# Moving one dense matmul ahead of the first weighing part in units 18 to 30, and reordering the tail's output products

## The chip, the core and the metric

The kernel runs on one core of a Trainium2 chip. The metric is device microseconds (us) of one execution; each time quoted is the median of several runs. TensorE does the matmuls, VectorE, ScalarE and GpSimd the elementwise work, and SyncE issues most DMAs.

## The reference, cut to what matters

```python
xn = layernorm(x)                                     # x: 1 x 2048 x 1024, bf16
return x + attention(xn, wq, wk, wv, wo, beta) + token_mlp(xn, w1, b1, w2, b2)

def attention(x, ...):                                # 32 heads of 32, four segments of 512 tokens
    for s in range(4):
        p = softmax(q_s k_s^T * scale + causal_mask)
        a_dot = p v_s                                 # inside the segment
        a_mem = phi(q_s) M / (phi(q_s) z + 1e-6)      # memory of the earlier segments
        outs.append(g * a_mem + (1 - g) * a_dot)      # g = sigmoid(beta), per head
        M, z = M + phi(k_s)^T v_s, z + sum(phi(k_s))
    return concat(outs) @ wo
# [... the token MLP: two matmuls with a gelu between ...]
```

## The kernel before

The token MLP runs first. The attention then goes through 32 *units*: a unit is one segment and one group of four heads. Each unit makes *score products* (TensorE), which ScalarE exponentiates and GpSimd masks. *Weighing* multiplies the masked weights by the values, and is done for the previous unit, in three parts (0, 1, 2), so that TensorE needn't wait. Between these stand *dense* matmuls (projections and output products, eight matmuls of 512 columns to a job), which depend on nothing recent and fill TensorE's waits. An even unit has a third score product, which covers blocks of two units.

TensorE writes to eight banks: 0 to 3 hold scores, 4 and 5 weighing results, 6 and 7 dense jobs in turn. A bank can be written again only when the engine that empties it has finished. One order of instructions is fixed for each engine when the program is built. A dense job of the output product is emptied by an addition on VectorE (`fin`), and a weighing part by a copy on VectorE (`ost`). VectorE works through them in the order in which they were emitted.

```python
    def wo_job(self, c, half):          # one output product: 8 matmuls, then an addition on VectorE
        # [... mm(b, j): matmul j of the job into bank b ...]
        def end(b):
            dst, R = self.fin[c % 4][:, half * 512:(half + 1) * 512], self.R_fin[c % 4][half]
            self.fw.op("dve", lambda e: e.tensor_tensor(dst, self.bank(b), dst.bitcast(F16), op=ALU.add),
                       reads=[self.R_bank[b], R], writes=[R])
            # [... with the second half: store to out, load the next fin ...]

    def dense(self, n, side=True):      # the next n dense matmuls
        # [... cut ...]
            with fw.group(reads=reads(), writes=[self.R_bank[b]]):
                for i in range(at, stop):
                    mm(b, i)
            if stop == 8:
                end(b)                  # the job is complete: its evacuation is emitted here
                self.jobs.popleft()

    def logits(self, u, step):          # score product: matmuls into banks 0 to 3, one exponential out of them
        # [... cut ...]
        reads = [R for v in units for R in (self.R_kT[v % 3], self.R_qT[v % 3])]
        with fw.group(reads=reads, writes=self.R_bank[0:4]):
            # [... four or eight matmuls of 32 rows ...]
        fw.op("act", lambda e: e.activation(dst, src, ACT.Exp, scale=SCALE), reads=self.R_bank[0:4], ...)
        # [... a causal mask on GpSimd for each diagonal block ...]

    def attention(self):
        # [... cut ...]
            if u < 10 or u >= 14 and total <= 26:
                cuts = self.cut(total, (0, 4, 2, 4, 1, 13, 8) if even else (7, 3, 2, 4, 1, 15))
            else:
                cuts = self.cut(total, (0, 4, 2, 2, 2, 14, 8) if even else (7, 3, 2, 2, 2, 16))
            self.dense(cuts[0])
            self.logits(u, 0)                        # first score product
            self.dense(cuts[1], end)
            self.weigh(u - 1, 0)                     # first weighing part
            self.dense(cuts[2], False)
            self.weigh(u - 1, 1)
            self.dense(cuts[3], False)
            self.weigh(u - 1, 2)                     # third part: the bank of part 0 again
            # [... VectorE's steps on the results, queued ...]
            self.dense(cuts[4])
            self.logits(u, 1)                        # second score product
            if even:
                self.dense(cuts[5])
                self.logits(u, 2)                    # third score product
            self.dense(...)                          # the rest
```

```python
    def _waits(self, es, reads, writes, extra=()):
        # [... need: one token for each semaphore, in the order in which it was met ...]
        for t in need.values():
            es.wait_tok(t)
```

After the last unit, the tail does the last segment's output products, numbered 0 to 7, into all eight banks. Slice 6 of each needs the DMA that transposes unit 30's output (`oT<-o_s` in the profile), and slice 7 needs unit 31's.

```python
        def product(n, j0, j1, cols=((0, 512),)):    # slices j0 to j1 of product n
            i, h, b = n // 2, n % 2, (0, 1, 2, 3, 6, 7, 5, 4)[n]
            # [... the matmuls; after slice 7 an addition on VectorE and a store ...]
        product(0, 0, 6)
        product(1, 0, 6)
        self.weigh(u, 0)
        self.weigh(u, 1)
        product(2, 0, 6)
        self.weigh(u, 2)
        # [... VectorE's steps of unit 31 ...]
        product(3, 0, 6)
        for n in range(3):
            product(n, 6, 7)
        product(4, 0, 7)
        self.o_transpose(u, 4)
        product(3, 6, 7)
        product(5, 0, 7)
        for n in range(6):
            product(n, 7, 8)
        product(6, 0, 8)
        product(7, 0, 8, ((0, 256), (256, 384), (384, 512)))
```

## Time and profile before

| | before |
|---|---|
| time, median of 3 runs (first measurement) | 654.29 us |
| span of the profiled execution | 652.22 us |
| first score product of unit 18 to that of unit 31 | 97.59 us |
| first score product of unit 31 to the start of the last matmul | 20.43 us |
| start of the last matmul to the end | 2.90 us |

These lines of the page of the kernel before give each engine's busy time (share of the span, count of instructions), the granted clock in 40 slices (9 is 90% or more), the queue of instruction fetches (packets, MB), and the engines' shares of the chain of work that ended last.

```profile
span 652.2 us, 11204 instructions
...
PE 646.7 (99%) x4611; PEld 303.1 (46%) x4611; DVE 439.9 (67%) x829; ACT 281.5 (43%) x305; POOL 154.9 (24%) x181
...
PEclk9999999999999999999999999999999999999999
...
q8 instruction: 36, 0.59, 0.4%
...
PE 90%; DVE 4%; DMA 2%; ACT 1%; POOL 1%; issue 1%; DVEq 0%
```

TensorE (PE) bounds the kernel: it is busy for 99% of the span at full clock. What can move the time is a gap between matmuls, or the end behind the last one.

These lines are the timeline of the kernel before: start, length, engine, line, operation, out<-in, count, and in brackets the idle time of that engine before it and its inferred releaser. They come from unit 20, from unit 26 (first score product and first weighing part) and from the tail. PEld is TensorE's weight load, SPq a DMA issue on SyncE.

```profile
547.90 0.74 DVE L1466 TENSOR_TENSOR o_s<-prod 128x512 bf16<-128x512 bf16 x1
...
548.56 0.56 DVE L1414 CAST ost<-ps_all 128x396 bf16<-128x396 f32 x1
...
549.04 0.68 DVE L1306 TENSOR_TENSOR fin<-ps_all,fin 128x512 bf16<-128x512 f32 x1
549.17 0.47 PEld L199 LDWEIGHTS ps_all<-vA,pT 128*128 128x128 bf16 x16 [0.42 <-DVE ost L1414]
...
588.48 1.88 ACT L1363 ACTIVATE pT<-ps_all 128x2048 bf16<-128x2048 f32 x1 [0.79 <-PE ps_all L199]
...
590.48 0.13 PEld L199 LDWEIGHTS ps_all<-qT,kT 32*128 32x128 bf16 x4 [0.49 <-issue]
590.50 0.40 PE L199 MATMUL ps_all<-qT,kT 32*128 32x512 bf16 x4
...
590.91 0.82 PE L199 MATMUL ps_all<-wv,xnT 128*128 128x512 bf16 x3
...
591.92 0.25 PE L199 MATMUL ps_all<-vA,pT 128*128 128x33 bf16 x4 [0.19 <-POOL pT L1367]
...
633.89 2.75 PE L199 MATMUL ps_all<-wo,oT 128*128 128x512 bf16 x12 [0.24 <-ACT pT L1363]
...
636.15 0.34 SPq L221 DMA_DIRECT2D out_dram<-fin  x1
636.53 0.92 SPq L221 DMA_DIRECT2D fin<-out_dram  x1
...
637.49 1.19 SPq L221 DMA_TRANSPOSE oT<-o_s  x1
...
640.46 0.98 PEld L199 LDWEIGHTS ps_all<-wo,oT 128*128 128x128 bf16 x6 [0.49 <-DMA oT<-o_s]
```

In unit 20, VectorE empties the bank of part 0 (548.56) directly behind `o_s`, then does the output addition; the third weighing part follows at 549.17. In unit 26 the first weighing part waits for GpSimd. In the tail TensorE waits for an exponential at 633.89 and for the transposing DMA at 640.46. A load's bracket holds more than a loss, because a load normally overlaps the matmul before it. The gaps quoted below are therefore starts of matmuls, less the 0.216 us that a matmul of 512 columns takes.

### The profile page before, as it was taken

How to read it: one execution, taken by the hardware profiler on the slowest of the kernel's cores; microseconds unless marked ns; L12 is line 12 of the kernel's file. 1: busy time of each engine (PE TensorE's matmuls, PEld its weight loads, DVE VectorE, ACT ScalarE, POOL GpSimd, SP SyncE). 2: the span in 40 equal slices, each digit the busy share in tenths (PEclk: the TensorE clock that was granted, in tenths of full speed). 3: DMA queues.
4: the chain of work that ended last, by engine and by line, in shares of the span. 5: the costliest groups of instructions: out<-in, count | busy, mean ns of one | idle time of the engine just before them, and what ended most of it. 6: DMA issues, size and time to landing. Idle time of an engine off the chain costs nothing.

```text
span 652.2 us, 11204 instructions
## 1 busy us (share of the span) xinstructions
PE 646.7 (99%) x4611; PEld 303.1 (46%) x4611; DVE 439.9 (67%) x829; ACT 281.5 (43%) x305; POOL 154.9 (24%) x181
## 2 busy tenths in 40 slices
PE   9999999999999999999999999999999999999998
PEld 3444444444444444444444444444545444454444
DVE  6975775665655673745637325767898988887895
ACT  7542232232210000111101047778767788888760
POOL 2500000000011220120201203434333445544450
PEclk9999999999999999999999999999999999999999
DMA  8804242242498937629263956979644576355424
GB/s 300 217 0 130 65 116 79 65 124 70 129 265 216 231 96 210 171 87 258 66 193 116 257 136 156 190 182 227 124 120 109 152 164 144 90 115 123 114 81 138
DMA packets 190123, 95.00 MB, mean 146 GB/s; under 512 B 108664, under 2 KB 176248, under 8 KB 190072
## 3 DMA queue, kind: packets, MB, share of 16 engines
q1 hardware_dynamic: 189928, 94.25, 56.9%
q8 instruction: 36, 0.59, 0.4%
q14 instruction: 15, 0.12, 0.1%
q10 hardware_dynamic: 144, 0.03, 0.0%
HBM read 69.23 MB, written 11.53 MB: 124 GB/s over the span
## 4 chain that ended last, share of the span: by engine, by line
PE 90%; DVE 4%; DMA 2%; ACT 1%; POOL 1%; issue 1%; DVEq 0%
PE ps_all L199 90%; ACT pT L1363 1%; DMA w2s<-in_B_w_dram 1%; POOL pT L1367 1%; DVE fin L1617 1%; DVE ln_st L590 1%; DVE sum L651 0%; DVE prod L1460 0%; DMA xin<-in_A_x_dram 0%; DVE h L630 0%; POOL ln_rs L614 0%; DVE mtmp L1229 0%; DVE mtmp L1227 0%; DVE ost L1414 0%; DVE part L692 0%
## 5 line engine op out<-in xcount | busy, mean ns | idle before, releaser
L1363 ACT ACTIVATE pT<-ps_all 128x2048 bf16<-128x2048 f32 x80 | 150.2, 1877 | 47.2 <-PE ps_all L199 46.8
L1367 POOL TENSOR_SCALAR_AFFINE_SELECT pT<-pT 128x512 bf16<-128x512 bf16 x128 | 106.3, 847 | 160.9 <-ACT pT L1363 160.9
L692 DVE TENSOR_TENSOR part<-ps_all,part 128x512 f32<-128x512 f32 x84 | 57.7, 690 | 108.9 <-PE ps_all L199 88.2
L1078 POOL TENSOR_TENSOR part<-part,stg 128x512 f32<-128x512 f32 x24 | 33.0, 1402 | 285.0 <-DVE part L692 268.1
L749 ACT ACTIVATE g<-part,b1c 128x512 f16<-128x512 f32 x36 | 26.0, 722 | 99.0 <-DVE part L692 99.0
L199 PE MATMUL ps_all<-wv,xnT 128*128 128x512 bf16 x256 | 68.2, 380 | 0.2
L199 PE MATMUL ps_all<-xnT,wq 128*128 128x512 bf16 x256 | 65.6, 380 | 0.0
L199 PE MATMUL ps_all<-wo,oT 128*128 128x512 bf16 (+2 forms) x272 | 64.3, 367 | 0.2 <-ACT pT L1363 0.2
L1414 DVE CAST ost<-ps_all 128x396 bf16<-128x396 f32 (+2 forms) x96 | 44.3, 473 | 27.3 <-PE ps_all L199 26.6
L697 ACT ACTIVATE part<-ps_all 128x512 f32<-128x512 f32 x24 | 14.0, 596 | 101.4 <-PE ps_all L199 67.1
L199 PEld LDWEIGHTS ps_all<-vA,pT 128*128 128x128 bf16 x1280 | 45.5, 96 | 21.5 <-DVE ost L1414 3.3
L199 PE MATMUL ps_all<-g,sum 128*128 128x512 f16 x224 | 51.0, 379 | 0.0
L199 PE MATMUL ps_all<-g,w2s 128*128 128x512 f16 x224 | 51.0, 379 | 0.0
L199 PE MATMUL ps_all<-gT,sum 128*128 128x512 f16 x224 | 50.3, 379 | 0.1
L199 PE MATMUL ps_all<-vA,pT 128*128 128x33 bf16 x1280 | 48.5, 178 | 0.7 <-POOL pT L1367 0.6
L199 PE MATMUL ps_all<-h,sum 128*128 128x512 f16 x192 | 45.2, 379 | 0.0
L199 PE MATMUL ps_all<-h,w1s 128*128 128x512 f16 x192 | 44.9, 379 | 0.0
L199 PE MATMUL ps_all<-hT,sum 128*128 128x512 f16 x192 | 43.6, 379 | 0.0
L199 PEld LDWEIGHTS ps_all<-wo,oT 128*128 128x128 bf16 x272 | 23.8, 97 | 27.1 <-issue 4.9
L1460 DVE TENSOR_TENSOR prod<-ost,srec 128x1024 bf16<-128x1024 bf16 x24 | 35.1, 1461 | 0.0
L199 PEld LDWEIGHTS ps_all<-gT,sum 128*128 128x128 f16 x224 | 21.8, 98 | 26.8 <-DVE gT L666 0.6
L199 PEld LDWEIGHTS ps_all<-g,w2s 128*128 128x128 bf16 x224 | 21.9, 98 | 26.4
(118 smaller groups left out, 862.2 us busy)
## 6 DMA issues: line engine op xcount, KB each, us to landing
w2s<-in_B_w_dram SPq DMA_DIRECT2D x8, 1792.0 KB, 9.5
w1s<-in_B_w_dram SPq DMA_DIRECT2D x12, 1024.0 KB, 5.6
wq<-in_A_wq_dram SPq DMA_DIRECT2D x32, 256.0 KB, 3.4
xs<-in_A_x_dram SPq DMA_DIRECT2D x24, 256.0 KB, 3.4
stg<-in_A_x_dram SPq DMA_DIRECT2D x16, 256.0 KB, 2.8
out_dram<-stg SPq DMA_DIRECT2D x16, 256.0 KB, 3.8
wk<-in_A_wk_dram SPq DMA_DIRECT2D x16, 256.0 KB, 3.4
fin<-out_dram SPq DMA_DIRECT2D x16, 256.0 KB, 3.3
```

Of the source, the lines that this page charges most:

```text
L199: ins = self.nc.tensor.matmul(*args, **kwargs)
L590: fw.op("dve", lambda e: e.bn_stats(st[:, 6 * h:6 * h + 6], src[:, 512 * h:512 * h + 512]), reads=[self.R_xin[c]], writes=[R])
L692: self.fw.op("dve", lambda e: e.tensor_tensor(self.tmp[dst][:], self.bank(b), self.tmp[src][:], op=ALU.add), reads=[self.R_bank[b], self.R ...
L697: self.fw.op("act", lambda e: e.activation(self.tmp[dst][:], self.bank(b), ACT.Copy), reads=[self.R_bank[b]], writes=[self.R_tmp[dst]])
L749: self.fw.op("act", lambda e: e.activation(self.gB[f % 2][half][:, f // 2, :], src, ACT.Gelu_apprx_tanh, bias=self.b1c[:, f:f + 1], scale= ...
L1078: fw.op("pool", lambda e: e.tensor_tensor(self.tmp[t][:], self.tmp[t][:], self.stg[k][:, 512 * half:512 * half + 512], op=ALU.add), reads= ...
L1363: fw.op("act", lambda e: e.activation(dst, src, ACT.Exp, scale=SCALE), reads=self.R_bank[0:4], writes=[R[v % 2][kb] for v, kb, _ in blocks ...
L1367: fw.op("pool", lambda e: e.affine_select(d, d, pattern=[[0, 4], [1, P]], compare_op=ALU.is_ge, fill=0.0, base=0, channel_multiplier=-1), ...
L1414: fw.op("dve", lambda e: e.tensor_copy(dst, src), reads=[self.R_bank[b]], writes=[self.R_ost[o][part]])
L1460: fw.op("dve", lambda e: e.tensor_tensor(self.prod[:], ost[:, :, 0:D_HEAD], rec.unsqueeze(2).to_broadcast([P, 32, D_HEAD]), op=ALU.mult), ...
L1617: fw.op("dve", lambda e: e.tensor_tensor(dst, self.ps[:, b, c0:c1], dst.bitcast(F16), op=ALU.add), reads=[self.R_bank[b], R], writes=[R])
```

## The change

The change has three parts. The first moves one filler matmul to where TensorE waits for GpSimd's masking in the even units from 18 on. The second puts the tail's first product into a dense bank that is idle by then, so that it needn't wait for the last exponential to leave bank 0. The third finishes products 0 to 4 before the last three slices of product 5, so that VectorE's final additions start earlier.

```diff
--- before.py
+++ after.py
@@ -1544,7 +1544,9 @@
             if u in self.XN_AT[::4]:
                 self.xn_load(xn)
                 self.xn_load(xn + 1)
-            if u < 10 or u >= 14 and total <= 26:
+            if u >= 18 and even:
+                cuts = self.cut(total, (0, 4, 1, 4, 0, 9, 6))
+            elif u < 10 or u >= 14 and total <= 26:
                 cuts = self.cut(total, (0, 4, 2, 4, 1, 13, 8) if even else (7, 3, 2, 4, 1, 15))
             else:
                 cuts = self.cut(total, (0, 4, 2, 2, 2, 14, 8) if even else (7, 3, 2, 2, 2, 16))
@@ -1603,7 +1605,7 @@
         fw.wait_outputs(3)
 
         def product(n, j0, j1, cols=((0, 512),)):
-            i, h, b = n // 2, n % 2, (0, 1, 2, 3, 6, 7, 5, 4)[n]
+            i, h, b = n // 2, n % 2, (6 + self.turn, 0, 1, 2, 3, 7 - self.turn, 5, 4)[n]
             for p, (c0, c1) in enumerate(cols):
                 with fw.group(reads=self.R_wo[j0:j1] + self.R_oT[s % 3][j0:j1], writes=[self.R_bank[b]]):
                     for jc in range(j0, j1):
@@ -1634,9 +1636,10 @@
         product(4, 0, 7)
         self.o_transpose(u, 4)
         product(3, 6, 7)
-        product(5, 0, 7)
-        for n in range(6):
+        product(5, 0, 5)
+        for n in range(5):
             product(n, 7, 8)
+        product(5, 5, 8)
         product(6, 0, 8)
         product(7, 0, 8, ((0, 256), (256, 384), (384, 512)))
```

No matmul is added or removed.

## The prediction

> **What bounds the kernel.** TensorE. The page shows it busy for 646.7 of 652.2 us at full granted clock; the chain of waits is 90% TensorE. Starts of consecutive 512-column matmuls lie 0.216 us apart in the trace, as the Trainium skill has it ("TensorE: Matmul & The Clock Gate", "Back-to-back issue gap"). No matmul is added or removed, so only gaps between matmul starts can change. I read those from the timeline.
>
> **Part 1, even units 18 to 30.** One dense matmul moves from behind the second score product (10 become 9) to ahead of the first weighing part (3 become 4). Gaps before:
> - Units 26, 28, 30: the first weighing part waits 0.35, 0.42, 0.35 us for GpSimd's masking (1.35 us after a 1.88 us exponential).
> - Units 18, 20, 24: the third weighing part waits 0.21, 0.09, 0.09 us for VectorE to empty its bank (ost eviction). Unit 22: no wait.
>
> Effect:
> - 26, 28, 30: 0.216 us of the masking wait is hidden. Behind it the third score product waits for the exponential: 0.44 + 1.88 + 0.14 = 2.46 us after the second, against 2.59 before and 2.38 of matmuls left. So 0.08 comes back; net gain 0.13 each.
> - 18: VectorE wait gone, 0.08 back: gain 0.13.
> - 22: about 0.09 lost.
> - 20, 24: the fourth matmul completes an output product before the weighing, so the output addition (0.68 us, 0.60 start to start) now stands ahead of the first ost eviction on VectorE, which is late there (unit 20: o_s ends 548.64, the eviction 549.11, the matmul starts 549.17). The eviction now ends near 549.71, the weighing starts near 549.77, against 549.29 if nothing held it. Loss about 0.48 each. The same swap in unit 28 is free: VectorE is idle there.
>
> Sum: 4 x 0.13 gained, 0.09 + 2 x 0.48 lost: 0.5 us slower.
>
> **Part 2, first tail product in the idle dense bank.** It removes the 0.41 us wait at 633.89 for the exponential that holds bank 0. But at 640.47 the seventh-slice products wait 0.16 us for the transposing DMA of unit 30's output, whose time is set by VectorE and the DMA queue (issued 637.49, landed 2.9 us later), not by these matmuls. This wait grows to about 0.57: gain about 0.
>
> **Part 3, product 5 split 7+1 into 5+3.** The final additions start two matmuls (0.43 us) earlier. VectorE does ten back to back from 645.00 to 650.00; the last can't start before the last matmul ends (649.54), against 649.73 now. Gain 0.15, perhaps 0.25 with the last store's issue, queued behind another. The copied transpose is ready at 643.66; its first user comes at 644.16, so no new wait.
>
> **Total.** 654.29 + 0.5 - 0.2: **654.5 us**, range 653.7 to 655.2. Faster by over 2%: 0.005; within 2%: 0.99; slower by over 2%: 0.005.
>
> **What would show it.** Units 26, 28, 30: masking wait 0.14 to 0.21, and a new gap of about 0.08 before the third score product. Units 20, 24: a gap of about 0.5 before the third weighing part, released by the ost eviction just behind the output addition. Tail: no gap for the exponential, but about 0.57 at the DMA of oT; additions 0.4 us earlier after the transpose, not all back to back at the end.
>
> **What would make it wrong.** VectorE finishing earlier in units 20 and 24 (products take 1.67 us there, beside GpSimd, against 1.22 later), which would turn the loss into a small gain and the time into about 653.6; the transposing DMA landing earlier: up to 0.4 us; or the exponential starting late behind a ScalarE copy where 9 matmuls are left: up to 0.1 us each.

(The last sum is loose: 654.29 + 0.5 - 0.2 is 654.6, not 654.5.)

## More of the kernel before

The next view is the windows view of the kernel before, cut at the score products of unit 18 and 31 and at the last matmul. After the stretch and its length it gives the busy time and count of each engine, then clock, DMA share and GB/s.

```profile
core 0: us, PE busy (x) PEld busy (x) DVE busy (x) ACT busy (x) POOL busy (x), PEclk, DMA share, GB/s
531.30:628.89 97.59, 96.66 (x1106) 47.76 (x1107) 81.94 (x161) 80.18 (x70) 47.11 (x54) 1.00 0.49 117
628.89:649.32 20.43, 20.19 (x197) 11.04 (x196) 14.77 (x29) 4.35 (x3) 3.83 (x5) 1.00 0.39 123
649.32:652.22 2.90, 0.22 (x4) 0.04 (x1) 0.68 (x3) 0.00 (x0) 0.00 (x0) 0.91 0.47 140
```

Those three stretches are where the change acts. The length of each is the figure to follow; the clock of 0.91 in the last is a halving from 651.7 us on, behind the last matmul, so it slows none.

All runs compared here are in the fast state (granted TensorE clock at full speed), apart from one outlier of 861 us among nine runs of the kernel before, which the ratios leave out.

## The result, and the profile after

Ratios are computed as the mean time of one kernel's fast runs over the mean of the other's of the same rounds, so they aren't quite the ratios of the medians. Executions over 1.5% slower than the fastest of the same kernel are left out of the means.

| | before | after | difference | predicted |
|---|---|---|---|---|
| median of 6 runs, us | 654.42 | 653.44 | -0.98 | +0.2 |
| ratio (95% interval) | | 0.9985 (0.9973 to 0.9998) | | |
| profiled span, us | 652.22 | 651.27 | -0.95 | |
| unit 18 to unit 31, us | 97.59 | 97.49 | -0.10 | +0.5 |
| unit 31 to last matmul's start, us | 20.43 | 20.22 | -0.21 | 0 |
| last matmul's start to the end, us | 2.90 | 2.51 | -0.39 | -0.15 to -0.25 |

The change is within 2%, as predicted, but the time fell, to 653.44 us, below the predicted range (653.7 to 655.2). The three stretches of this pair of profiles sum to -0.70. The other 0.25 us of the spans' difference is a wait for a weight DMA at 183 us in the profile of before (0.24 us), far ahead of the change. The first score product of unit 0 came at 387.48 us there and at 387.23 in after, but at 387.61 in a repeat of the changed kernel, which shows the same wait (0.23 us), so that difference is chance.

The page of the kernel after:

```profile
span 651.3 us, 11204 instructions
...
PE 95%; DVE 3%; issue 1%; DMA 0%; ACT 0%
```

ScalarE and GpSimd, 1% each of the chain before, have all but left it. The windows of the kernel after, with the same cuts and columns:

```profile
531.05:628.54 97.49, 96.58 (x1106) 47.88 (x1107) 82.06 (x161) 80.04 (x70) 47.52 (x54) 1.00 0.48 117
628.54:648.76 20.22, 20.03 (x196) 11.15 (x196) 15.37 (x30) 4.35 (x3) 3.85 (x5) 1.00 0.40 128
648.76:651.27 2.51, 0.22 (x4) 0.05 (x1) 0.40 (x2) 0.00 (x0) 0.00 (x0) 1.00 0.45 131
```

The timeline of the kernel after, at the answering places (unit 20, the first weighing part and the third score product of unit 26, the tail):

```profile
547.44 0.73 DVE L1466 TENSOR_TENSOR o_s<-prod 128x512 bf16<-128x512 bf16 x1
...
548.10 0.68 DVE L1306 TENSOR_TENSOR fin<-ps_all,fin 128x512 bf16<-128x512 f32 x1
...
548.70 1.03 DVE L1414 CAST ost<-ps_all 128x396 bf16<-128x396 f32 x2
549.31 0.47 PEld L199 LDWEIGHTS ps_all<-vA,pT 128*128 128x128 bf16 x16 [0.80 <-DVE ost L1414]
...
591.22 1.04 PE L199 MATMUL ps_all<-wv,xnT 128*128 128x512 bf16 x4
...
592.23 0.25 PE L199 MATMUL ps_all<-vA,pT 128*128 128x33 bf16 x4
...
595.10 1.88 ACT L1363 ACTIVATE pT<-ps_all 128x2048 bf16<-128x2048 f32 x1 [0.43 <-PE ps_all L199]
...
597.03 0.12 PEld L199 LDWEIGHTS ps_all<-qT,kT 32*128 32x128 bf16 x8 [0.43 <-ACT pT L1363]
597.03 0.40 PE L199 MATMUL ps_all<-qT,kT 32*128 32x256 bf16 x8
...
635.80 0.34 SPq L221 DMA_DIRECT2D out_dram<-fin  x1
636.18 0.66 SPq L221 DMA_DIRECT2D fin<-out_dram  x1
...
636.89 1.19 SPq L221 DMA_TRANSPOSE oT<-o_s  x1
...
639.91 1.62 PEld L199 LDWEIGHTS ps_all<-wo,oT 128*128 128x128 bf16 x9 [0.68 <-DMA oT<-o_s]
```

In unit 20 the output addition now stands ahead of the evacuation, and the third weighing part is held, as predicted. In unit 26 the first weighing part comes four dense matmuls after the score product instead of three, and its wait falls from 0.35 to 0.14 us. The third score product of unit 26 starts 0.06 us after its exponential ends (595.10 + 1.88 = 596.98), where the prediction had 0.14. In the tail the wait for the exponential is gone, and the load of `fin` now holds SyncE's queue for 0.66 us instead of 0.92.

The lengths of the even units, from first score product to first score product, in us:

| unit | 18 | 20 | 22 | 24 | 26 | 28 | 30 |
|---|---|---|---|---|---|---|---|
| before | 9.05 | 8.93 | 8.97 | 8.93 | 9.02 | 9.02 | 9.04 |
| after | 8.84 | 9.31 | 8.98 | 9.31 | 8.80 | 8.81 | 8.81 |
| difference | -0.21 | +0.38 | +0.01 | +0.38 | -0.22 | -0.21 | -0.23 |
| predicted | -0.13 | +0.48 | +0.09 | +0.48 | -0.13 | -0.13 | -0.13 |

Every unit is about 0.09 us better than predicted. That is one error, made seven times.

### The profile page after: what moved, and what is told of

Its sections match the earlier page's. It is cut to its first block, busy times and chain, and to the rows that moved or that the text cites. A ratio compares the mean times of both kernels' runs of the same rounds, so it can differ in the third digit from the quotient of the medians.

```text
span 651.3 us, 11204 instructions
## 1 busy us (share of the span) xinstructions
PE 646.3 (99%) x4611; PEld 303.5 (47%) x4611; DVE 440.4 (68%) x829; ACT 281.3 (43%) x305; POOL 155.4 (24%) x181
## 4 chain that ended last, share of the span: by engine, by line
PE 95%; DVE 3%; issue 1%; DMA 0%; ACT 0%
PE ps_all L199 95%; DVE prod L1460 1%; DMA oT<-o_s 0%; DVE ost L1414 0%; DVE fin L1306 0%; ACT pT L1363 0%; DVE mtmp L1229 0%; DVE mtmp L1227 0%; DVE o_s L1466 0%; DVE srec L1456 0%; DVE MZbf L1424 0%; DVE pqT L1229 0%; DVE MZ L1422 0%; DVE kT L1261 0%; DVE srec L1457 0%
## 5 line engine op out<-in xcount | busy, mean ns | idle before, releaser
L199 PEld LDWEIGHTS ps_all<-g,sum 128*128 128x128 f16 x224 | 21.9, 98 | 26.4
```

Of the source, the lines that this page charges most:

```text
L199: ins = self.nc.tensor.matmul(*args, **kwargs)
```

## The experiments

All kernels gave correct results. "Time" is the median, and "before" is the median of the kernel before in the same rounds on the same chip. A difference of half a microsecond lies inside the interval of a ratio here (about 0.13%, or 0.9 us, to each side), so the stretches of the traces decide on such sizes, and the times only support them. No kernel here differs from the one before by as much as 2%.

### Repeat, and the three parts alone

`after_again` is the changed kernel once more; the other three are the kernel before with one of the three parts of the diff above.

> The changed kernel once more, as the measure for the other runs, and to see how much of its trace repeats. If the first profile was typical: units 18 to 30 (first score product of unit 18 to first score product of unit 31) take 97.49 us as before, against 97.59 in the kernel before; unit 20 and 24 take 9.31 us, units 18, 26, 28, 30 8.81 to 8.84 us; from unit 31 to the last matmul 20.22 us against 20.43. If the 0.25 us by which the first profile was already ahead at unit 0 is chance (one 0.24 us stall at 183 us, waiting for weights, in the profile of before alone), it comes and goes with the runs; a rival, that the change moves something in the first half, wants it in every run of the changed kernel. Time about 0.7 to 0.95 us below before.

> Part 1 alone. Theory (read from the changed kernel's trace, against my prediction): the third score product follows the exponential with no new gap, so units 18, 26, 28, 30 gain 0.21 us each and units 20 and 24 lose 0.38 each; units 18 to 30 take 97.49 us, 0.10 less than before, and the time falls by 0.1 only. The theory of the prediction (0.08 us comes back in each unit) wants these units 0.5 us longer than before and the time 0.5 us up.

```diff
+            if u >= 18 and even:
+                cuts = self.cut(total, (0, 4, 1, 4, 0, 9, 6))
```

> Part 2 alone. Theory of the prediction: the 0.41 us wait for the exponential goes, and the wait for the transposing DMA of unit 30's output grows from 0.16 to 0.57 us, so the tail from unit 31 to the last matmul stays at 20.43 us and the time stays. Rival: the DMA was sooner in the changed kernel because of this part (issued 8.35 us after unit 31's first score product against 8.60), the wait grows only to 0.35 and the tail takes 20.2 us; the time falls by 0.2.

```diff
-            i, h, b = n // 2, n % 2, (0, 1, 2, 3, 6, 7, 5, 4)[n]
+            i, h, b = n // 2, n % 2, (6 + self.turn, 0, 1, 2, 3, 7 - self.turn, 5, 4)[n]
```

> Part 3 alone. The last matmul comes no sooner (20.43 us after unit 31 begins), but the final additions start 0.43 us earlier against it. Theory of the prediction: the span behind the last matmul's start (2.90 us before) shrinks by 0.15 to 0.25. What the changed kernel's trace showed: it shrinks by 0.35 (to 2.54), the store behind the last addition no longer queued behind another store's issue. Time down by 0.15 to 0.35.

```diff
-        product(5, 0, 7)
-        for n in range(6):
+        product(5, 0, 5)
+        for n in range(5):
             product(n, 7, 8)
+        product(5, 5, 8)
```

| kernel | time | against before (654.42) | ratio (95%) | 18 to 31 | 31 to last matmul | last matmul to end |
|---|---|---|---|---|---|---|
| after_again | 653.50 | -0.92 | 0.9989 (0.9975 to 1.0002) | 97.48 | 19.90 | 2.52 |
| only_cuts | 654.28 | -0.14 | 0.9998 (0.9985 to 1.0011) | 97.47 | 20.37 | 2.91 |
| only_bank | 654.04 | -0.38 | 0.9995 (0.9982 to 1.0008) | 97.59 | 20.24 | 2.91 |
| only_split | 654.02 | -0.40 | 0.9994 (0.9982 to 1.0007) | 97.59 | 20.76 | 2.51 |

The three differences sum to -0.92, the time of the whole; with intervals of 0.9 us on each, so close an agreement is luck. Part 1 shortens the units by 0.12 us, and part 3 the end by 0.39. Part 2 gains something, where the prediction had nothing, but the stretch that it should shorten varies from one profile to another (20.24 here, 19.90 in the repeat). Part 3 alone has 20.76 there, although its diff only reorders matmuls late in that stretch. Something that the diff doesn't name acts in the tail.

### turn_step2 and turn_step0: which wait an instruction itself carries

The first score product (step 0) and the third (step 2) each wait for two semaphores, ScalarE's exponential (the banks are free) and the DMA of the keys, landed long before. In the trace's instruction records, step 0 has a separate event-semaphore instruction on TensorE's queue that waits for ScalarE (at 590.398 for unit 26 of before, 0.051 us long). The weight load behind it carries the DMA's wait. At step 2 it is the other way round: the load itself waits for ScalarE. The theory: this order alone makes the first product start 0.145 us after its exponential and the third 0.056. The rival: the two products differ in shape (32x512 against 32x256, four against eight matmuls) or in what ScalarE does meanwhile. The Trainium skill ("Perfetto Trace Analysis", "Identifying Dependency Chains") says that an instruction that waits for several engines may have event-semaphore instructions put ahead of it; the trace agrees, with 0.051 us for one.

Both kernels are the changed kernel with the order of waits turned round at chosen groups. Nothing is taken away from what is waited for.

```diff
-        for t in need.values():
+        for t in (list(need.values())[::-1] if turn else need.values()):
             es.wait_tok(t)
 # turn_step2, in logits:
-        with fw.group(reads=reads, writes=self.R_bank[0:4]):
+        with fw.group(reads=reads, writes=self.R_bank[0:4], turn=step == 2 and u >= 18):
 # turn_step0 has, in logits, turn=step == 0 and u >= 18, and in weigh:
-        with fw.group(reads=reads, writes=[self.R_bank[b]]):
+        with fw.group(reads=reads, writes=[self.R_bank[b]], turn=part == 0 and u >= 17):
```

> The changed kernel, with the order of two waits turned at the third score product of units 18 to 30 (its matmuls wait for ScalarE's exponential and for a DMA of k; the DMA has long landed). Theory W: TensorE waits for the first of the two in an instruction of its own and for the second at the weight load; where the exponential is the second, the product may follow it by 0.056 us, where it is the first (as at the first score product of the even units, from which the prediction took its 0.14) by 0.145. So here the product comes 0.145 us after the exponential ends, its gap grows from 0.10 to 0.19 us in all seven even units, units 18 to 30 take 98.1 us against 97.48 and the time rises by 0.6. Rival: the 0.145 belongs to the first score product (its width, its place), then nothing changes.

> The changed kernel, with the order of two waits turned at the first score product of each unit (exponential, then DMA of k: now the DMA first) and at the first weighing part (GpSimd, then VectorE: now VectorE first). Theory W: the gap ahead of the first score product falls from 0.19 to 0.10 us in units 20 to 30; the first weighing part follows the masking by 0.06 instead of 0.14 us. Net gain 0.08 to 0.09 in units 22, 26, 28, 30, none in 20 and 24, where VectorE decides: units 18 to 30 take 97.1 to 97.2 us against 97.48, time down by 0.3. Rival as in the run before: no change.

| kernel | time | against before (654.71) | ratio (95%) | 18 to 31 |
|---|---|---|---|---|
| turn_step2 | 654.54 | -0.17 | 0.9996 (0.9983 to 1.0009) | 98.11 |
| turn_step0 | 653.51 | -1.20 | 0.9982 (0.9969 to 0.9994) | 97.26 |

The waits view for TensorE's loads from unit 18 on (total us, times, longest) counts a load by the releaser that it shows. First after, then turn_step2, then turn_step0:

```profile
PEld ps_all L199 <- issue: 13.4, 48, 0.5
PEld ps_all L199 <- ACT pT L1363: 6.0, 14, 0.4
```

```profile
PEld ps_all L199 <- issue: 16.8, 55, 0.5
PEld ps_all L199 <- ACT pT L1364: 3.0, 7, 0.4
```

```profile
PEld ps_all L199 <- ACT pT L1364: 8.9, 21, 0.4
PEld ps_all L199 <- issue: 8.8, 38, 0.5
...
PEld ps_all L199 <- POOL pT L1368: 1.3, 3, 0.5
```

Seven loads go from "ACT pT" to "issue" when step 2 is turned, and seven come the other way when step 0 is (three more go from "issue" to "POOL pT": the turned weighing parts). So "issue" ahead of a load is here no sign that it waited for nothing. It can mark a load whose late wait stood in the instruction ahead of it.

Timeline of turn_step2, the third score product of unit 26:

```profile
595.81 1.88 ACT L1364 ACTIVATE pT<-ps_all 128x2048 bf16<-128x2048 f32 x1 [0.43 <-PE ps_all L199]
...
597.80 0.15 PEld L199 LDWEIGHTS ps_all<-qT,kT 32*128 32x128 bf16 x8 [0.49 <-issue]
597.83 0.40 PE L199 MATMUL ps_all<-qT,kT 32*128 32x256 bf16 x8
```

The same product, of the same shape, now starts 0.145 us after its exponential (0.056 in after), with the bracket that the first product has in before. The stretch becomes 98.11 us, which is 97.59 + 0.52: the predicted size. With this edit, the arithmetic of part 1 comes true, so its latency was the error and the rest of it was right. The rival is out.

turn_step0 shows the same in reverse. The first product starts 0.055 us after its exponential and the masking wait of units 26 and 30 falls to about 0.05. In unit 28 that wait stays at 0.21 us, because the matmuls ahead of it came sooner as well; there the weighing part follows the masking by 0.056 us, where it was 0.147, so the short latency shows in a plain wait too. The stretch fell by 0.23 us to 97.26, where 97.1 to 97.2 was expected, a partial miss. In units 20 and 24 the earlier start only lengthens the wait for VectorE (0.47 to 0.57), and in units 22, 26 and 30 the next dense matmul waits 0.09 us longer for its bank, held by a ScalarE copy. In unit 22 nothing makes up for that: this is the miss.

### fin_late: the order on VectorE in units 20 and 24

The addition that the completed dense job emits is held back until the evacuation of the first weighing part has been emitted.

```diff
             if stop == 8:
-                end(b)
+                if self.hold is None or not on_dve:
+                    end(b)
+                else:
+                    self.hold.append((end, b))
 # [... attention(): hold is a list over self.dense(cuts[1], end) in even units from 18 ...]
                 self.weigh(u - 1, 0)
+            for job_end, b in held:
+                job_end(b)
```

> The changed kernel, with the output addition that became ready before the first weighing part handed to VectorE behind that part's ost eviction (units 20, 24, 28), as in the kernel before; TensorE's order is untouched. Theory: the 0.475 us gap before the third weighing part in units 20 and 24 is the output addition ahead of the eviction; it goes to 0, both units take 8.84 us instead of 9.31, units 18 to 30 take 96.5 us against 97.48, and the time falls by 0.95. Rival: VectorE is late there anyway (its products take 1.67 us), and a gap of 0.1 to 0.2 stays.

Measured: 652.60 us against 654.71, -2.11, ratio 0.9969 (0.9955 to 0.9983). Unit 18 to 31 took 96.51 us, as expected, and units 20 and 24 took 8.83 each. The timeline of fin_late in unit 20:

```profile
548.35 0.56 DVE L1417 CAST ost<-ps_all 128x396 bf16<-128x396 f32 x1
...
548.83 0.68 DVE L1306 TENSOR_TENSOR fin<-ps_all,fin 128x512 bf16<-128x512 f32 x1
548.95 0.58 PEld L199 LDWEIGHTS ps_all<-vA,pT 128*128 128x128 bf16 x16 [0.21 <-DVE ost L1417]
```

The evacuation is again ahead of the addition, and the load of the third part follows it with the 0.21 us bracket of an ordinary stream. The loss predicted for units 20 and 24 was real and had the cause named. It was 0.97 us for the two units, about as much as the whole change gained.

### The tail: TensorE's instruction fetch and SyncE's queue

The prediction held that the transposing DMA's time doesn't depend on TensorE's matmuls. VectorE's part of that was right. Counted from unit 31's first score product, `o_s` ended at 7.56 us before (636.04 + 0.41 - 628.89) and at 7.57 after, and the issue of the load of `fin` began at 7.64 and 7.65. But that issue lasted 0.92 us before and 0.66 after, and the transposing DMA stands behind it on SyncE's queue.

The page has a queue of instruction fetches with 36 packets. In the trace's DMA records each is of 16,384 bytes, and those after the first lie 255 TensorE records apart on average. That fits the Trainium skill ("Runtime: NRT & Kernel Launch", "Instruction fetch mechanics"), which says that an engine's instructions come in blocks of 16 KiB, 256 instructions, through a DMA queue of their own, at a cost "mostly hidden". One such packet falls in the tail. (That the queue is TensorE's is inferred from this spacing; the shifts below agree.) The theory: while it is under way, the issue of the load of `fin` doesn't complete. TensorE fetches sooner when it isn't held by the exponential, so the DMA comes sooner too. The rival: the issue varies by itself, or with traffic of other DMAs.

Two experiments move the packet without touching the tail, by changing the number of warm-up matmuls at the program's start, whose results nobody reads. `tail_order` instead leaves the packet alone and puts filler ahead of the slices that need the DMA.

```diff
 # fetch_early: 60 more TensorE instructions
-            for _ in range(self.N_WARM):
-                fw.mm(self.bank(0), self.warm[:, 0:P], self.warm[:], start=True, stop=True)
+            for n in [512] * 5 + [128] * 40:
+                fw.mm(self.bank(0)[:, 0:n], self.warm[:, 0:P], self.warm[:, 0:n], start=True, stop=True)
 # fetch_late: 6 fewer
-    N_WARM = 15
+    N_WARM = 12
 # tail_order
-        for n in range(3):
+        product(4, 0, 6)
+        for n in (0, 1, 2, 4):
             product(n, 6, 7)
-        product(4, 0, 7)
```

> The changed kernel, with 10 of the 15 warming matmuls cut in four: 60 more TensorE instructions in the same time, so that TensorE's later instruction fetches (16 KB DMA packets) come 60 instructions sooner; in unit 31 about 4 us sooner. Theory F: in all six profiles the load of fin just ahead of the transposing DMA ends its issue 0.38 us after the end of the fetch packet of TensorE's instructions (at 7.6 to 8.6 us in unit 31) unless that is earlier than its plain length of 0.44; part 2 gained because TensorE, no longer waiting for the exponential, fetches 0.4 us sooner. So with the fetch out of the way the load's issue takes 0.44 us, the transposing DMA is issued 8.13 us after unit 31 begins (8.35 and 8.13 in the two profiles of the changed kernel, 8.60 before), TensorE waits for it not at all and unit 31 to the last matmul takes 19.87 us, in every profile. Rival: the issue time is chance or other traffic, and stays between 0.44 and 1.3 us.

> The changed kernel with 12 warming matmuls instead of 15: 6 TensorE instructions fewer, so that the fetch in unit 31 comes three dense matmuls (0.65 us) later. Theory F: the fetch packet ends at 8.3 to 9.2 us in unit 31 instead of 7.6 to 8.1, the load of fin ends its issue 0.38 us behind that, the transposing DMA is issued 8.7 to 9.6 us after unit 31 begins, TensorE waits for it 0.7 to 1.5 us and unit 31 to the last matmul takes 20.6 to 21.4 us against 19.9 to 20.5. Rival (traffic or chance): no different from the changed kernel. The start may be some tenths slower or faster for its own reasons; read the tail alone.

> The changed kernel with the first six slices of tail product 4 moved ahead of the seventh slices of products 0 to 2, in place of behind them: six more matmuls (1.3 us) before TensorE needs the transposing DMA of unit 30's output. Theory: that wait (0, 0.18, 0.35, 0.59 us in profiles so far, by when the fetch fell) goes in every case, unit 31 to the last matmul takes 19.87 us, and the time falls by 0.2 to 0.3. Rival: the wait only moves to the transpose of unit 31's output behind it, which needs VectorE's o_s (ready at 641.47 in the changed kernel, 0.6 us ahead of TensorE); then a gap stays there.

The table gives, for every profile with the old tail order, times in us from unit 31's first score product: the fetch packet's start and end, the end of the issue of the load of `fin`, the issue of the transposing DMA, TensorE's wait for it, and the start of the last matmul. The first three have product 0 in bank 0, the others in the idle dense bank.

| kernel | fetch packet | load's issue ends | DMA issued | wait | last matmul |
|---|---|---|---|---|---|
| before | 7.31 to 8.18 | 8.56 | 8.61 | 0.16 | 20.43 |
| only_cuts | 7.00 to 8.17 | 8.55 | 8.60 | 0.09 | 20.37 |
| only_split | 7.17 to 8.57 | 8.93 | 8.98 | 0.49 | 20.76 |
| only_bank | 6.92 to 7.86 | 8.24 | 8.28 | 0.37 | 20.24 |
| after | 6.64 to 7.93 | 8.31 | 8.35 | 0.35 | 20.22 |
| after_again | 6.70 to 7.62 | 8.09 | 8.13 | about 0.02 | 19.90 |
| turn_step2 | 6.63 to 7.61 | 8.08 | 8.13 | 0.18 | 20.05 |
| turn_step0 | 6.73 to 8.09 | 8.47 | 8.52 | 0.58 | 20.46 |
| fin_late | 6.69 to 7.62 | 8.08 | 8.13 | 0.08 | 19.95 |
| fetch_early | 3.95 to 4.89 | 8.09 | 8.13 | 0.13 | 20.00 |
| fetch_late | 7.28 to 8.51 | 8.88 | 8.92 | 0.93 | 20.80 |

Where the packet ends after about 7.7, the load's issue ends 0.36 to 0.38 us after the packet, in all six such rows of the unmoved program and in fetch_late. Where the packet is done by then or far away, the issue takes its plain 0.44 us and the DMA goes out at 8.13. The same holds outside the tail. From unit 18 on, the 14 traces have 701 issues on SyncE's queue that transpose nothing. All 55 that took over 0.65 us had such a packet under way and ended 0.20 to 0.46 us after it (median 0.38). The relation isn't complete: an issue can pass under a packet unstretched, as the store ahead of the load does in the tail (0.34 us), and earlier in the program long issues occur without a packet (1.23 us at 395.7 us of before). The timeline of fetch_late in the tail:

```profile
636.20 0.34 SPq L221 DMA_DIRECT2D out_dram<-fin  x1
636.58 1.23 SPq L221 DMA_DIRECT2D fin<-out_dram  x1
...
637.85 1.19 SPq L221 DMA_TRANSPOSE oT<-o_s  x1
...
640.88 0.55 PEld L199 LDWEIGHTS ps_all<-wo,oT 128*128 128x128 bf16 x4 [1.26 <-DMA oT<-o_s]
```

The same load takes 1.23 us to issue, and TensorE then stands for 0.93 us ahead of the seventh slices. Times: fetch_late 654.28 us against 654.61 (-0.33, ratio 0.9995, 0.9976 to 1.0014, two runs), and fetch_early 653.69 against 654.71 (-1.02, 0.9988, 0.9975 to 1.0000). fetch_late met its expectation. In fetch_early the packet came 2.8 us sooner than on average in the six rows above it, where about 4 was expected. It met its expectation for the issue (8.13), but a wait of 0.13 stayed where none was expected, because the DMA landed later after the same issue. That spread of landings isn't explained.

The mean stretch is 20.52 us in the first three rows (20.37 to 20.76) and 20.14 in the six rows that have the bank change and the program's own warm-up (19.90 to 20.46). The difference of 0.38 rests on few profiles, whose ranges overlap; that only_bank's time fell by 0.38 too proves nothing, with an interval of 0.9. Between the same rows the packet's mean start went from 7.16 to 6.72 and the DMA's mean issue from 8.73 to 8.26, and of these two the ranges don't overlap. The mean wait for the DMA stayed (0.25 and 0.26).

tail_order took 653.20 us against 654.61 (-1.41, ratio 0.9979, 0.9966 to 0.9992). Its packet ended at 8.01 and its load's issue at 8.38, as the relation has it, but TensorE no longer waits, and the last matmul starts at 19.87, as expected.

What holds up SyncE's issue during the fetch is only argued. The Trainium skill ("DMA: Bandwidth & Descriptors", "Queues, rings and completion order") says that each DMA engine takes turns between the queues that it serves, packet by packet, which would fit if the load's work stood behind the packet on one engine. The records used here don't tell the engines apart, so no run shows that.

### all4 and all5: the findings together

all4 is the changed kernel with the edits of turn_step0, fin_late and tail_order. all5 also moves one more dense matmul ahead in units 26 to 30:

```diff
-                cuts = self.cut(total, (0, 4, 1, 4, 0, 9, 6))
+                cuts = self.cut(total, (0, 5, 1, 3, 0, 9, 6) if u >= 26 else (0, 4, 1, 4, 0, 9, 6))
```

> The changed kernel with three repairs together: the order of waits at the first score product and first weighing part, the output addition behind the ost eviction, and the tail order. If they add: units 18 to 30 take 97.48 - 0.97 - 0.22 = 96.3 us, unit 31 to the last matmul 19.87, and the time is 1.2 to 1.5 us below the changed kernel, 2.2 to 2.5 below the kernel before.

> As all4, and in units 26 to 30 a fifth dense matmul ahead of the first weighing part, taken from those just behind it, so that the third score product keeps its distance. It should hide what is left of the masking wait (0.05, 0.21, 0.05 us in units 26, 28, 30 with the waits in the better order): 0.3 us less than all4, units 18 to 30 take 96.0 us. Rival: the masking comes later by as much, and nothing is gained.

| kernel | time | against before (654.61) | ratio (95%) | 18 to 31 | 31 to last matmul |
|---|---|---|---|---|---|
| all4 | 651.69 | -2.92 | 0.9957 (0.9944 to 0.9970) | 96.10 | 19.87 |
| all5 | 651.44 | -3.17 | 0.9952 (0.9938 to 0.9966) | 95.77 | 19.86 |

all4 gained more than expected (96.3 us for units 18 to 31, and 2.2 to 2.5 us in all), because two repairs help each other: with VectorE's wait gone from units 20 and 24, the earlier first score product is no longer lost there (both take 8.83 us, 9.41 and 9.40 in turn_step0). all5 gained its 0.3 us more. It beats both kernels: 3.17 us against the kernel before, three times what the change gave.

## Why the prediction was wrong, point by point

- **TensorE bounds the kernel, and only gaps and the end can change: right.** The three stretches of the repeat changed by -0.11, -0.53 and -0.38 us against the first profile of before, which together is the timed difference within 0.1 us. The figure of 0.216 us for a matmul of 512 columns, which the prediction took from the trace, held in all profiles.
- **Part 1, the masking wait: right.** In units 26, 28 and 30 the waits after were 0.14, 0.21 and 0.14 us, as predicted.
- **Part 1, units 20 and 24: right in mechanism and size.** The addition came ahead of the evacuation, and the third weighing part waited 0.475 and 0.473 us (0.48 predicted). fin_late shows the cause by removing it.
- **Part 1, "behind it the third score product waits for the exponential: 0.44 + 1.88 + 0.14": this step failed.** The term 0.14 was the mis-sized one; it measured 0.056. It had been read off the first score product, whose wait for ScalarE stands in an instruction ahead of the load. In the third, the load itself carries that wait. With 0.056 the exponential is ready in time: the gap ahead of the third product is 0.10 us (0.098 to 0.100), hardly more than at a switch from matmuls of 128 rows to matmuls of 32 rows where nothing is waited for (0.096). The seven units were therefore 7 x 0.09 = 0.6 us too slow in the prediction, and its +0.5 became -0.1. turn_step2 shows it: with the waits turned, 98.11 us.
- **Part 2, "whose time is set by VectorE and the DMA queue, not by these matmuls": this step failed too.** VectorE's time was indeed unmoved (7.56 and 7.57), but the queue's was not. One of TensorE's instruction fetches delays an issue on SyncE's queue, and the fetch follows TensorE's progress. The wait did not grow to 0.57; it measured 0.35 in this profile, and over the profiles it kept its mean (0.25 and 0.26). The gain was 0.21 us in this profile and 0.38 on average over few profiles, not 0. The prediction had listed an earlier landing of this DMA, "up to 0.4 us", among what would make it wrong, but without a cause. How the fetch holds up the issue stays open.
- **Part 3: right in mechanism, too small in size.** The gain was 0.39 us, not 0.15 to 0.25. The last addition ended 0.14 us sooner after the last matmul's start (0.55, was 0.69), which is the predicted 0.15. The last store's issue came another 0.13 sooner behind it, because SyncE no longer was busy with the store before; the prediction allowed 0.10. The last store then took 1.93 us instead of 2.05; that 0.12 was in no term, and its cause wasn't tested.
- **The sum.** Against the predicted parts, 0.6 us comes from the wait order, 0.2 to 0.4 from the tail's DMA and 0.15 to 0.2 from the end. Together that is 0.95 to 1.2 us. The timed distance is 1.2 us, between +0.2 and -0.98, of which 0.1 is the loose sum of the prediction; the rest is within the noise. The prediction also named 653.6 us for the case that VectorE finishes earlier in units 20 and 24. That this is near the measured 653.44 is luck, because VectorE did not (waits of 0.475 and 0.473 us).

## What to carry to other kernels

Take a release latency only from an instruction that waits in the same form: where a group waits for two semaphores, put the one that comes late last, so that the instruction itself carries it (0.09 us at each such wait here, of which the next wait took back a part). When filler moves ahead of a critical step, look at which jobs it completes, because their evacuations enter another engine's queue ahead of the critical one (0.48 us each here, and free to avoid). Removing a stall also moves the engine's instruction fetches; if a DMA issue close to the critical path varies from profile to profile, compare it with them, and put independent work ahead of its user.

## What the Trainium skill lacked or had wrong

- "TensorE: Matmul & The Clock Gate", "Back-to-back issue gap": it puts 216 ns for 512 columns down to isolated matmuls and about 131 ns to a real stream of weight loads and matmuls. This kernel is such a stream, at full granted clock, and every profile shows 0.216 us from start to start of consecutive matmuls of 512 columns.
- "Perfetto Trace Analysis", "Identifying Dependency Chains": it names the event-semaphore instructions put ahead of an instruction, but not that the order of the waits has a price. Here the start after the release is 0.145 us when the late wait is in the instruction ahead and 0.056 us when it is in the weight load itself.
- "Runtime: NRT & Kernel Launch", "Instruction fetch mechanics": the blocks of 256 instructions agree, but "mostly hidden" left out a cost. A packet in the tail took 0.9 to 1.4 us, and one that ended late stretched a DMA issue of another queue from 0.44 to as much as 1.29 us, and TensorE's wait behind it to 0.93 us. No page was found that connects the two.
- "TensorEngine Tiling (Array Packing)", "Key Properties": it says that a change of tiling mode drains TensorE, without a figure. Here the switch from matmuls of 128 rows to matmuls of 32 rows shows a gap of 0.096 us.
